# Moving the transposes of W2 from TensorE to the DMA engines, beside a stream of loads

## The chip, the cores and the metric

The kernel runs on one core of a Trainium2 chip. The metric is the device time of one execution, in microseconds (us); smaller is better. The profile's span is a little shorter than this time: 172.3 us of span go with about 174 us. A run is called slow when it lies over 1.5% above the fastest of the same kernel, and ratios use fast runs alone.

## The reference, cut to what matters

Sinkhorn-normalised block attention for four items of 8 heads and 768 tokens, followed by a maxout layer:

```python
x = attention(q, k, v, sort_net)      # (3072 tokens, 512)
h1 = x @ w1                           # w1, w2: (512, 1024)
h2 = x @ w2
g = np.maximum(h1, h2)
out = g @ w_out                       # w_out: (1024, 512)
```

The kernel uses max(h1, h2) = h2 + relu(h1 - h2). So it needs only relu(x (W1 - W2)) for every token, and x (W2 Wout) for the rest. W2 Wout is a 512x512 product that is made once; its left operand must stand in memory as W2 transposed.

## The kernel before

These are the parts that the change and the argument touch. An engine that waits holds up what stands behind it in its own program, as VectorE's first g shows in the result below (45.72 us, behind the turns of v at 43.44). All loads are issued by GpSimd, in one queue; they cast float32 to bf16 on the way.

```python
load_v(0, 0, 3)
...
load_k(0); load_q(0)
load_w_columns(w2_sb, moe_w2, 0, 2)        # W2, first half of the columns
load_w_columns(w1_sb, moe_w1, 0, 1)
load_w_columns(w1_sb, moe_w1, 1, 2)
load_w_columns(w2_sb, moe_w2, 2, 4)        # W2, second half
load_w_columns(w1_sb, moe_w1, 2, 4)        # the last columns of W1
load_w(wo_sb, moe_w_out)
load_v(1)                                  # item 1
w_difference(0, nc.gpsimd)                 # W1 - W2, first quarter
load_k(1)
```

The transposes of W2 are 32 TensorE instructions in two groups, each with one eviction from PSUM, and the product reads the result:

```python
def w2_transposes(t, eng):
    ps = ps_bf16("tw_ps")
    for n in range(16):
        fb, dmt = t * 4 + n // 4, n % 4
        nc.tensor.matmul(ps[:, n * 128 : (n + 1) * 128],
            w2_sb[:, dmt, fb * 128 : (fb + 1) * 128], ident, is_transpose=True, ...)
    return lambda: evac(w2T[:, t * 4 : t * 4 + 4, :]..., ps, 2048, two_x=True, eng=eng)

def w_product(dmt, eng=None):              # one of four "W products"
    for fb in range(NFB):                  # NFB = 8
        nc.tensor.matmul(wc_ps[0][...], w2T[:, fb, dmt * 128 : (dmt + 1) * 128],
                         wo_sb[:, fb, :], ...)
```

For item 0 the order of units is: h of the first half of the tokens, two W products, h of the second half (four products, `moe_h(0, 1, 0..3)`), the other two W products, then the output products. `turn` brings item 1's v into another layout on VectorE in eight pieces; each waits for the load of v.

The softmax here doesn't subtract the row's maximum and nothing guards it: scores larger than these inputs give would overflow.

## Time and profile before

| | before |
|---|---|
| time, median (lowest to highest) | 173.39 us (172.95 to 173.56, 3 runs) |
| TensorE busy | 161.7 us, 94% of the span |
| loads | 12.58 MB written, stream full from 3 to 57 us |
| TensorE transposes of W2 | 32, in two groups of about 1 us |
| DMA transposes (x and q of items 1 to 3) | 16, all after 59 us |

The chain of waits says which engine the end was waiting for, step by step, as shares of the span:

```profile
PE 79%; DMA 7%; ACT 6%; POOL 2%; DVE 2%; issue 2%; ACTq 0%; POOLq 0%
```

PE is TensorE. It is the bound, and DMA stands only for the first load of q.

### The profile page before, as it was taken

The page shows a single profiled execution, that of the slowest core. Times are in us where ns is not written, and L with a number is a line of the kernel's source. Part 1 is how long each engine was busy: PE and PEld are TensorE (multiplying, and loading weights), DVE is VectorE, ACT ScalarE, POOL GpSimd, SP SyncE. Part 2 cuts the span into 40 slices and gives each one's busy share as a digit, 9 for nine tenths or more (in the row PEclk, how much of TensorE's full clock was granted, in tenths as well). Part 3 has the DMA queues.
Part 4 walks back from the last instruction along what each step waited for, and adds up shares of the span by engine and source line. Part 5 has one row for each costly group of instructions (what it writes and reads, how often), then busy time and mean ns, then how long its engine had stood idle before and what let it go on. Part 6 is the DMA issues. An engine that isn't in the chain of part 4 may idle for free.

```text
span 172.3 us, 4531 instructions
## 1 busy us (share of the span) xinstructions
PE 161.7 (94%) x1997; PEld 98.1 (57%) x2015; DVE 88.4 (51%) x194; ACT 83.8 (49%) x101; POOL 24.5 (14%) x40
## 2 busy tenths in 40 slices
PE   7899999989999999998989899999999999999990
PEld 7847766735666555456655445575554546654470
DVE  5879677679656399810685255044452422320130
ACT  4599875864745554069971532465605404312000
POOL 7953362251300000000600000000000000000000
PEclk9999999999999999999999999999999999999998
DMA  3999999999999352993497549920035173000342
GB/s 49 201 206 207 199 207 210 207 205 207 220 212 199 60 167 51 166 233 122 58 203 117 101 135 203 182 109 4 0 51 147 37 198 125 0 0 0 122 183 65
DMA packets 29811, 23.11 MB, mean 134 GB/s; under 512 B 16672, under 2 KB 24736, under 8 KB 29792
## 3 DMA queue, kind: packets, MB, share of 16 engines
q0 software_dynamic: 10304, 12.58, 42.9%
q1 hardware_dynamic: 19200, 10.04, 23.2%
q8 instruction: 16, 0.26, 0.6%
q10 hardware_dynamic: 288, 0.20, 0.4%
q14 instruction: 3, 0.02, 0.0%
HBM read 25.17 MB, written 6.29 MB: 183 GB/s over the span
## 4 chain that ended last, share of the span: by engine, by line
PE 79%; DMA 7%; ACT 6%; POOL 2%; DVE 2%; issue 2%; ACTq 0%; POOLq 0%
PE out_ps L603 36%; PE h_ps L576 24%; DMA q_raw<-in_q_dram 7%; PE o_ps L473 5%; PE wc_ps L554 4%; PE s_ps L446 3%; PE k_ps L379 2%; ACT kT L104 2%; ACT g L590 1%; DVE g L592 1%; ACT w2T L104 1%; PE tw_ps L531 1%; PE tq_ps L349 1%; PE tq_ps L354 1%; POOL k_raw L145 1%
## 5 line engine op out<-in xcount | busy, mean ns | idle before, releaser
L603 PE MATMUL out_ps<-wo_sb,g 128*128 128x512 bf16 (+2 forms) x197 | 47.0, 362 | 1.1 <-ACT o L104 0.5
L576 PE MATMUL h_ps<-xT,w_sb 128*128 128x384 bf16 x256 | 44.8, 326 | 0.8 <-DVE g L592 0.6
L576 PEld LDWEIGHTS <-w_sb 128*128 128x128 bf16 x256 | 24.2, 97 | 16.3 <-issue 0.6
L454 ACT ACTIVATE e<-s_ps 96x768 bf16<-96x768 f32 x32 | 24.2, 807 | 15.8 <-PE s_ps L446 15.7
L603 PEld LDWEIGHTS <-g 128*128 128x128 bf16 x208 | 17.7, 97 | 15.9 <-issue 0.5
L590 ACT ACTIVATE g<-h_ps 128x768 bf16<-128x768 f32 x22 | 17.8, 813 | 16.4 <-PE h_ps L576 16.4
L104 ACT COPY o<-out_ps 128x1024 f32<-128x1024 f32 x10 | 10.1, 1012 | 31.4 <-PE out_ps L603 31.4
L603 PE MATMUL out_ps<-wc,xT 128*128 128x512 bf16 (+2 forms) x103 | 24.9, 362 | 0.1
L490 DVE TENSOR_TENSOR x<-o_ps,rs 96x512 bf16<-96x512 f32 x32 | 22.0, 687 | 1.1
L592 DVE TENSOR_SCALAR g<-h_ps 128x768 bf16<-128x768 f32 x10 | 9.6, 958 | 15.9 <-PE h_ps L576 15.6
L484 DVE RECIPROCAL rs<-o_ps 96x8 f32<-96x8 f32 x32 | 6.4, 201 | 21.7 <-PE o_ps L473 21.5
L603 PEld LDWEIGHTS <-xT 128*128 128x128 bf16 x104 | 9.9, 97 | 11.0
L211 DVE COPY v_dc<-v_raw 64x768 bf16<-64x768 bf16 (+2 forms) x18 | 15.5, 902 | 0.4 <-DMA v_raw<-in_v_dram 0.3
L473 PEld LDWEIGHTS <-e 96*128 96x128 bf16 x256 | 11.6, 97 | 6.6 <-DVE x L490 0.5
L106 DVE CAST v_sb<-v_ps 96x1024 bf16<-96x1024 f32 x7 | 8.5, 1215 | 11.8 <-PE v_ps L421 8.4
L473 PE MATMUL o_ps<-v_sb,e 96*128 96x65 bf16 x256 | 13.1, 193 | 0.1
L104 ACT CAST v_sb<-v_ps 96x1024 bf16<-96x1024 f32 x9 | 8.7, 1014 | 2.0 <-PE v_ps L400 1.9
L446 PEld LDWEIGHTS <-kT 64*128 64x128 bf16 x256 | 6.0, 94 | 6.2 <-issue 4.2
L446 PE MATMUL s_ps<-qT,kT 64*128 64x96 bf16 x256 | 8.7, 204 | 0.7 <-ACT kT L104 0.6
L104 ACT CAST kT<-k_ps 128x1024 bf16<-128x1024 f32 x9 | 8.6, 1021 | 0.7 <-PE k_ps L379 0.7
L82 PEld LDWEIGHTS <-fill 128*128 128x128 bf16 x109 | 7.6, 128 | 2.2 <-DVE fill L73 1.2
L554 PE MATMUL wc_ps<-wo_sb,w2T 128*128 128x512 bf16 x29 | 7.4, 380 | 0.7 <-ACT w2T L104 0.5
(76 smaller groups left out, 130.0 us busy)
## 6 DMA issues: line engine op xcount, KB each, us to landing
out_dram<-o SPq DMA_DIRECT2D x11, 512.0 KB, 3.0
k_raw<-in_k_dram POOLq DMA_DIRECT2D x12, 256.0 KB, 10.4
q_raw<-in_q_dram POOLq DMA_DIRECT2D x4, 768.0 KB, 12.6
v_raw<-in_v_dram POOLq DMA_DIRECT2D x6, 384.0 KB, 13.6
w_sb<-in_moe_w_dram POOLq DMA_DIRECT2D x3, 512.0 KB, 15.9
wo_sb<-in_moe_w_out_dram POOLq DMA_DIRECT2D x2, 512.0 KB, 19.4
v_raw<-in_v_dram POOLq DMA_DIRECT2D x3, 256.0 KB, 4.9
w_sb<-in_moe_w_dram POOLq DMA_DIRECT2D x2, 256.0 KB, 14.3
```

What stands on the lines that cost most here:

```text
L104: nc.scalar.copy(out=out_ap, in_=in_ap)
L106: nc.vector.tensor_copy(out=out_ap, in_=in_ap)
L211: nc.vector.tensor_copy(out=dst, in_=src)
L446: nc.tensor.matmul(ps[:, h2 * 512 + ii * 128 : h2 * 512 + ii * 128 + BLK], kT[b][rows, (hp * 8 + i) * BLK : (hp * 8 + i) * BLK + 128], rhs ...
L454: nc.scalar.activation(out=e[:, 0 : 8 * BLK].rearrange("p (t c r) -> p t c r", t=8, r=R), in_=ps[0:BLK].rearrange("p (t f) -> p t f", t=8) ...
L473: nc.tensor.matmul(ps[:, h2 * 512 + ii * 65 : h2 * 512 + (ii + 1) * 65], e[:, (h2 * 4 + ii) * BLK : (h2 * 4 + ii) * BLK + 128], v_sb[:, m0 ...
L490: nc.vector.tensor_tensor(out=x, in0=ov[:, :, :, 0:D], in1=rs.to_broadcast([BLK, 2, 4, D]), op=ALU.mult,)
L554: nc.tensor.matmul(wc_ps[0][:, m * 512 : (m + 1) * 512], w2T[:, fb, dmt * 128 : (dmt + 1) * 128], wo_sb[:, fb, :], start=(fb == 0), stop=( ...
L576: nc.tensor.matmul(h_ps[t][:, m * 512 : m * 512 + TCH], w1_sb[:, hp, fb * 128 : (fb + 1) * 128], xT[:, b % 2, ch, hp % 2, hp // 2, :], sta ...
L590: nc.scalar.activation(out=g, in_=src, func=AF.Relu)
L592: nc.vector.tensor_scalar(out=g, in0=src, scalar1=0.0, scalar2=None, op0=ALU.max)
L603: nc.tensor.matmul(dst, g_tiles[b, ch, m // 2][:, m % 2, off : off + 128] if m < NFB else xT[:, b % 2, ch, hp % 2, hp // 2, off : off + 12 ...
```

## The change

Its intent is to take 32 transposes off the bounding engine, and two evictions off VectorE and ScalarE. W2 is transposed by eight DMA transposes on the SP queue, which has nothing else to do then. Since they land later, all four W products move behind item 0's h products. The rest spreads the turns of v over the new units and drops a loop that ran once.

```diff
-    w2T = big.tile([128, NFB, DMODEL], BF16, tag="w2T", name="w2T")
+    w2T = big.tile([128, HP, NFB, 128], BF16, tag="w2T", name="w2T")
-    def w2_transposes(t, eng):
-        ... (16 TensorE transposes into PSUM, one eviction)
+    def w2_transposes(t):
+        for dmt in range(HP):
+            nc.sync.dma_start_transpose(
+                out=w2T[:, dmt, t * 4 : t * 4 + 4, :],
+                in_=w2_sb[:, dmt, t * 512 : (t + 1) * 512],
+            )
...
-    w2_out = w2_transposes(0, "D")
-    w2_out()
+    w2_transposes(0)
+    w2_transposes(1)
...
         3: [
             VA[6],
-            lambda: w2_transposes(1, "A")(),
             VA[7],
             lambda: x_transposes(0, 2, "A"),
+            lambda: x_transposes(0, 3, "A"),
             lambda: [turn(second, c) for c in (0, 12, 24)],
         ],
-        4: [lambda: x_transposes(0, 3, "A"), load_rest, lambda: turn(second, 36)],
+        4: [load_rest, lambda: turn(second, 36), lambda: turn(second, 48)],
... (the other turns one unit earlier)
-        if b == 0:
-            units += wps[:2]
         units += [lambda t=t: moe_h(b, 1, t) for t in range(4)]
         if b == 0:
-            units += wps[2:]
+            units += wps
```

More of the change, by code (lines that the diff above doesn't have):

```diff
@@ L12 @@
 BF16 = mybir.dt.bfloat16
-TWICE = 1
 @with_exitstack
@@ L206, in turn_v @@
         src = v_raw[rows].rearrange("p (c d) -> p d c", d=D)[:, d0:d1, c0:c1]
-        for _ in range(TWICE):
-            if eng == "A":
-                nc.scalar.copy(out=dst, in_=src)
-            else:
-                nc.vector.tensor_copy(out=dst, in_=src)
+        if eng == "A":
+            nc.scalar.copy(out=dst, in_=src)
+        else:
+            nc.vector.tensor_copy(out=dst, in_=src)
     rowsum = const.tile([G, NB], FP32, tag="rowsum", name="rowsum")
@@ L521, in x_transposes @@
         evac(xT[:, b % 2, ih, hh], src, 2 * TCH, eng=eng)
-    w2T = big.tile([128, NFB, DMODEL], BF16, tag="w2T", name="w2T")
+    w2T = big.tile([128, HP, NFB, 128], BF16, tag="w2T", name="w2T")
     wc = big.tile([128, HP, DMODEL], BF16, tag="wc", name="wc")
-    def w2_transposes(t, eng):
-        ps = ps_bf16("tw_ps")
-        for n in range(16):
-            fb, dmt = t * 4 + n // 4, n % 4
-            nc.tensor.matmul(
-                ps[:, n * 128 : (n + 1) * 128],
-                w2_sb[:, dmt, fb * 128 : (fb + 1) * 128],
-                ident,
-                is_transpose=True,
-                start=True,
-                stop=True,
-            )
-        return lambda: evac(
-            w2T[:, t * 4 : t * 4 + 4, :].rearrange("p f d -> p (f d)"),
-            ps,
-            2048,
-            two_x=True,
-            eng=eng,
-        )
+    def w2_transposes(t):
[3 more added lines that the diff above has]
+                in_=w2_sb[:, dmt, t * 512 : (t + 1) * 512],
+            )
     wc_ps = {}
@@ L555, in w_product @@
                 wc_ps[0][:, m * 512 : (m + 1) * 512],
-                w2T[:, fb, dmt * 128 : (dmt + 1) * 128],
+                w2T[:, dmt, fb, :],
                 wo_sb[:, fb, :],
@@ L716 @@
             VA[6],
-            lambda: w2_transposes(1, "A")(),
             VA[7],
             lambda: x_transposes(0, 2, "A"),
+            lambda: x_transposes(0, 3, "A"),
             lambda: [turn(second, c) for c in (0, 12, 24)],
         ],
-        4: [lambda: x_transposes(0, 3, "A"), load_rest, lambda: turn(second, 36)],
-        5: [lambda: block_diagonals(1), lambda: turn(second, 48)],
-        6: [lambda: turn(second, 60)],
-        7: [lambda: turn(second, 72)],
-        8: [lambda: turn(second, 84)],
+        4: [load_rest, lambda: turn(second, 36), lambda: turn(second, 48)],
+        5: [lambda: block_diagonals(1), lambda: turn(second, 60)],
+        6: [lambda: turn(second, 72)],
+        7: [lambda: turn(second, 84)],
         9: [
@@ L754 @@
         if b == 0:
-            units += wps[2:]
-            cost[4:4] = [1.7] * 2
-            cost += [1.7] * 2
+            units += wps
+            cost += [1.7] * 4
         units += [
```

## The prediction

> **What bounds the kernel now.** I first read the page's busy shares and slices, to see which engine is full and until when memory is.
>
> ```profile
> PE 161.7 (94%) x1997; PEld 98.1 (57%) x2015; DVE 88.4 (51%) x194; ACT 83.8 (49%) x101; POOL 24.5 (14%) x40
> ...
> PE   7899999989999999998989899999999999999990
> ...
> DMA  3999999999999352993497549920035173000342
> GB/s 49 201 206 207 199 207 210 207 205 207 220 212 199 60 167 51 166 233 122 58 203 117 101 135 203 182 109 4 0 51 147 37 198 125 0 0 0 122 183 65
> ```
>
> TensorE is busy 94% of 172.3 us, so the end moves by TensorE work removed minus TensorE idle added. One slice is 4.3 us: the DMA engines are full up to about 56 us. So loads are the second bound there. The 200 to 220 GB/s are bytes as written in bf16; the loads cast from float32, so twice that is read (the page: 25.17 MB read, 12.58 MB moved by the load queue).
>
> Then I read the timeline of 16 to 44 us, where the changed work sits.
>
> ```profile
> 25.10 0.80 ACT L104 COPY xT<-tx_ps 128x768 bf16<-128x768 bf16 x1 [0.54 <-PE tx_ps L511]
> 25.42 1.04 PEld L531 LDWEIGHTS <-w_sb 128*128 128x128 bf16 x16
> ...
> 26.68 1.23 DVE L106 COPY w2T<-tw_ps 128x2048 bf16<-128x2048 bf16 x1 [1.81 <-PE tw_ps L531]
> ...
> 27.82 0.68 DVE L191 TENSOR_TENSOR w_sb<-w_sb 128x1024 bf16<-128x1024 bf16 x1
> ...
> 28.56 1.48 PE L576 MATMUL h_ps<-xT,w_sb 128*128 128x384 bf16 x8
> ...
> 32.47 1.06 PE L531 MATMUL tw_ps<-ident,w_sb 128*128 128x128 bf16 x16
> ...
> 33.56 1.87 ACT L104 COPY w2T<-tw_ps 128x2048 bf16<-128x2048 bf16 x1 [0.33 <-PE tw_ps L531]
> ...
> 35.07 3.04 DVE L211 COPY v_dc<-v_raw 64x768 bf16<-64x768 bf16 x4 [0.34 <-DMA v_raw<-in_v_dram]
> ...
> 35.48 1.04 PE L554 MATMUL wc_ps<-wo_sb,w2T 128*128 128x512 bf16 x4 [0.51 <-ACT w2T L104]
> ...
> 38.66 5.37 PE L576 MATMUL h_ps<-xT,w_sb 128*128 128x384 bf16 x32
> ...
> 40.38 0.96 DVE L592 TENSOR_SCALAR g<-h_ps 128x768 bf16<-128x768 f32 x1
> ```
>
> The reader is to see three things. Both W2 transposes cost TensorE about 1 us each, and their evictions 1.23 us of VectorE and 1.87 us of ScalarE. The third h product starts at 28.56, just after the W1 - W2 difference that it reads ended at 27.82 + 0.68 = 28.50. And VectorE's turning of item 1's v starts at 35.07 because v has only just landed. In the trace's landing records the last W1 columns land at 27.13 and v's first half at 35.05, so two consumers have almost no slack.
>
> The third view was the DMA issues, for what a transpose by DMA costs here.
>
> ```profile
> xT<-x SPq DMA_TRANSPOSE x12, 2.9
> ...
> qT<-q_pair SPq DMA_TRANSPOSE x4, 4.0
> ```
>
> **What the Trainium skill says.** "DMA: Bandwidth & Descriptors", section "Issuing engines are not separate DMA queues": transfers issued from SP and from GpSimd run on the same 16 engines and interleave. Its section "Queues, rings and completion order" has each engine go round its queues packet by packet. Before's trace has no moment with transposes beside a full load queue, so it can't confirm either. "Advanced Engine Details and Errata", section "X-Bar Transpose (TRN2)", says such transposes are as fast as regular DMAs, 350 to 400 GB/s. This trace disagrees: an x transpose of 768 packets of 256 B (197 KB) takes 1.15 us from first to last packet, 171 GB/s, and a packet 18 ns (median). "TensorE: Matmul & The Clock Gate", section "Part 4: PE-mode transpose", gives about 275 ns in a kernel for 128x128; here each lasts 217 ns, but 16 take only 1.06 us because they overlap. So what is removed is small.
>
> **The change, part by part.**
>
> *Removed.* 32 TensorE transposes: 0.89 and 0.91 us on the chain, 1.8 us. The stall of 0.51 us before the second four W products. 3.1 us of evictions, which no longer stand before the W1 - W2 difference and the xT eviction.
>
> *The first saving does not reach h.* Without the first 16 transposes, TensorE goes on after the xT eviction ends (25.10 + 0.80 = 25.90) instead of at 26.48: 0.55 us early, so it would reach the third h product at 28.0. But W1's last columns land at 27.13, the difference takes 0.7, so the product is allowed at about 27.95. There is no room for a later landing.
>
> *The second saving is lost in the new order.* Values 6 and 7 now follow each other, then both x transposes, then h at once. VectorE needs 0.9 us (0.2 reciprocal, 0.69 product) for each of the two x. Call T the start of the third h product. From the rows before, TensorE ends values 6 at T + 4.05, values 7 at T + 4.4, the first x transposes at T + 4.9; VectorE ends the second x at T + 5.95, so TensorE idles 1.1 us; the transposes end at T + 6.5, their eviction on ScalarE at T + 7.35, and the third matmul of h waits 0.55 us for it. The W products, which covered this eviction, are gone from here. h of the second half (four of 1.33 us) ends at T + 12.4, two W products (16 x 0.217 = 3.5) at T + 15.9, sorting k at T + 17.6, the third W product at T + 19.3. With T = 28.0 that is 47.3; before, TensorE stood at the same point at 47.42. So if the transposes cost the loads nothing, the change is worth about 0.1 us here. I worked out the choice of engine by the kernel's own load counter; it shifts a few evictions (all three kT of item 1 to ScalarE), worth some tenths either way.
>
> *Added: 1 MB by DMA amid the loads.* Eight transposes of 128x512: 512 packets each, 4096 in all, 256 per engine. At 18 to 25 ns a packet (25 is the pace of the two q transposes back to back, 3072 packets in 4.8 us) this is 4.6 to 6.4 us of every engine. If only the read side is short, 1 MB at the loads' read rate of 410 GB/s is 2.4 us. I choose 3 to 4. The first four can go when W2's first half has landed (19.38), the others when the second half has (24.55, later itself): all compete before v's first half lands.
>
> *On the path.* Half the delay, d1 = 1.5 to 2, shifts the last W1 columns, so T becomes 29.5 to 30. All of it, dv = 3 to 4, shifts v: the turning starts at 38 to 39. Three turns (2.35 us) now stand before the first g of the second half on VectorE, so this g ends at 38.5 + dv. The fourth h product needs its PSUM buffer (four in the ring) and gets there at T + 11.1 = 39.0 + d1. Further stall: dv - d1 - 0.5. Sum: the loss is the larger of d1 - 0.1 and dv - 0.6, which for dv = 3 is 2.4 us, for 4 is 3.4. Later everything is TensorE-bound and shifts along. The later loads' consumers (q of item 1 lands at 43.97, k at 40.02) come after the shifted W products and don't add.
>
> **Rivals.**
>
> (a) *The transposes slip between the loads.* If engines mostly wait for HBM, the loads lose under 1 us and the time is 173 to 174. For: packets of loads overlap in one engine (their durations sum to 1.2 times the slices). Against: the GB/s row is flat near 205 for packets from 512 to 4096 B, a rate that looks like a ceiling.
>
> (b) *The transposes starve.* If an engine alternates one small packet with one load packet (6144 B for v), the loads lose less early, but the last transposes land after 50 us and the last W products (50.05 before, some 52 then) wait: 177 to 179. For: the load queue is never empty up to 56 us. Against: the loads of W and q have short packets, so most transposes would pass with them.
>
> (c) *A gain.* The 1.8 us of TensorE work comes off in full and the x chain is hidden: 171.5. For: TensorE is the bound. Against: both savings end in front of a landing and a VectorE chain just computed. Over 2% (3.5 us) is more than all that is removed (1.8 + 0.5).
>
> **Range and chances.** The main line gives 173.4 + 2.4 to 3.4, about 176. Rival (a) and partial overlap pull it down; since the author re-spread the turns to suit, I lean that way and say 175.3. The range goes from (a)'s good end to (b)'s middle, 172.9 to 178.2. Slower by over 2% needs above 176.9, that is dv above 4 or (b): 0.28. Faster by over 2%: 0.02. The rest: 0.70.
>
> **What would show it.** Right: the transposes' landing times spread over 22 to 35 us; the last W1 columns land at 28.5 or later and the third h product starts behind them; VectorE's first turn waits for v until 37 to 39; a TensorE gap before the x transposes and before the fourth h product. Wrong: v landing within 1 us of 35.05, or W products waiting for w2T, or TensorE idle falling in 25 to 45 us.

## More of the kernel before

The next view gives, for stretches of the kernel, each engine's busy time in us and the number of its instructions, the granted clock of TensorE (1.00 is full), the busy share of the DMA engines (over 1 where packets overlap) and the GB/s that they moved:

```profile
core 0: us, PE busy (x) PEld busy (x) DVE busy (x) ACT busy (x) POOL busy (x), PEclk, DMA share, GB/s
...
44.00:56.00 12.00, 11.49 (x233) 8.09 (x236) 7.21 (x9) 6.99 (x8) 1.58 (x2) 1.00 1.11 210
56.00:68.00 12.00, 11.89 (x129) 6.18 (x130) 9.23 (x18) 6.40 (x8) 0.00 (x0) 1.00 0.43 99
68.00:76.00 8.00, 7.94 (x56) 4.08 (x56) 5.47 (x17) 1.97 (x3) 0.00 (x0) 1.00 0.96 190
```

TensorE is all but full in each stretch, at the full clock; in the first stretch the loads move at 210 GB/s. One row of the same timeline, the sorting of item 1's v (start and duration in us), serves as a mark for the comparison below:

```profile
47.43 1.57 PE L400 MATMUL v_ps<-bd,v_dc 64*128 64x64 bf16 x48
```

## The result

| | before | after |
|---|---|---|
| time, median | 173.47 us (172.95 to 173.8) | 198.8 us (197.99 to 199.17) |
| ratio | 1 | 1.1457 (95%: 1.1409 to 1.1504) |
| mean granted clock | 0.996 | 0.947 |

A ratio is the mean time of one kernel's fast runs over that of the other's of the same rounds, so not quite the ratio of the two medians. The change costs 25 us, and the predicted range ended at 178.2.

The page of the changed kernel: busy shares, then the slices of the span (each 4.9 us here; PEclk is TensorE's granted clock in tenths).

```profile
PE 167.1 (85%) x1983; PEld 98.1 (50%) x1983; DVE 87.1 (44%) x193; ACT 82.1 (42%) x100; POOL 23.2 (12%) x40
...
PE   7799969635670199999998899899999999999993
...
PEclk9999999985999556999999999999999999999999
DMA  4999999999999991033992792497202227200223
GB/s 71 206 200 202 206 170 198 142 130 133 198 190 188 99 110 25 0 91 100 174 196 88 112 202 51 146 177 183 95 3 41 44 106 186 106 3 0 106 87 125
...
PE 57%; DMA 19%; SPq 12%; ACT 5%; POOL 2%; issue 1%; DVE 1%; ACTq 0%; POOLq 0%
PE out_ps L589 32%; PE h_ps L562 14%; SPq L528 12%; DMA w2T<-w_sb 12%; DMA w_sb<-in_moe_w_dram 7%; PE o_ps L471 3%; PE wc_ps L540 3%; ACT kT L103 2%; PE s_ps L444 2%; PE v_ps L398 1%; ACT g L576 1%; PE tq_ps L347 1%; DVE g L578 1%; POOL k_raw L144 1%; POOL v_raw L153 1%
```

The damage lies between 25 and 75 us. The DMA row is full (9) to the fifteenth slice, as if much were moved, yet GB/s falls from 200 to 142, 130 and 133: the DMA engines had packets under way all the time and moved less. The last two lines are the chain of waits: the issue of the transposes on SP and their transfer, 12% each, have come into it, 24% of 197 us. Stretch by stretch, against the same stretches of before:

```profile
44.00:56.00 12.00, 6.59 (x24) 2.58 (x23) 7.72 (x14) 0.81 (x1) 2.44 (x5) 0.75 1.31 170
56.00:68.00 12.00, 2.88 (x102) 1.90 (x100) 0.44 (x1) 3.76 (x4) 0.93 (x1) 0.82 1.22 161
68.00:76.00 8.00, 7.67 (x69) 5.03 (x70) 3.40 (x3) 1.01 (x1) 0.00 (x0) 0.50 1.19 90
```

From 56 to 68 us TensorE works 2.9 us of 12. From 68 to 76 it looks busy again (7.67 of 8), but at a clock of 0.50: its matmuls take twice as long. The timeline names what it waited for (start, duration, engine, line, operation, output and inputs; in brackets the idle time before and what ended it):

```profile
19.74 32.33 SPq L528 DMA_TRANSPOSE w2T<-w_sb  x8
...
29.61 1.47 PE L562 MATMUL h_ps<-xT,w_sb 128*128 128x384 bf16 x8 [1.75 <-DVE w_sb L190]
...
35.74 0.51 PE L509 MATMUL tx_ps<-ident,x 96*128 96x96 bf16 x8 [1.27 <-DVE x L488]
...
43.44 2.25 DVE L209 COPY v_dc<-v_raw 64x768 bf16<-64x768 bf16 x3 [7.75 <-DMA v_raw<-in_v_dram]
...
45.72 0.96 DVE L578 TENSOR_SCALAR g<-h_ps 128x768 bf16<-128x768 f32 x1
...
46.73 2.72 PE L562 MATMUL h_ps<-xT,w_sb 128*128 128x384 bf16 x8 [5.61 <-DVE g L578]
...
55.24 1.04 PE L540 MATMUL wc_ps<-wo_sb,w2T 128*128 128x512 bf16 x4 [1.86 <-DMA w2T<-w_sb]
...
68.33 1.89 PE L540 MATMUL wc_ps<-wo_sb,w2T 128*128 128x512 bf16 x4 [9.44 <-DMA w2T<-w_sb]
...
70.15 2.74 PE L398 MATMUL v_ps<-bd,v_dc 64*128 64x64 bf16 x48
```

Two waits stand out. First, v of item 1 lands at 43.4 us instead of 35.05, VectorE turns it late, the first g of the second half stands behind these turns, and TensorE waits 5.61 us for that g's PSUM buffer. Second, the third W product waits 9.44 us for its transposed W2. The sorting of v, which began at 47.43 before, begins at 70.15 and takes 2.74 us instead of 1.57. From there on the two kernels do the same work.

The trace also holds every packet of the DMA engines and every landing. The following is worked out from these records (the packets of the load queue and of the transposes that start in each stretch of 4 us; 4-byte packets left out):

```
us            before: loads            after: loads             after: transposed
              packets  GB/s            packets  GB/s            packets (256 B each)
26 to 30      806      208             594      152             579
34 to 38      397      204             131      136             150
50 to 54      312      200             545      163             536
58 to 62       20        4             120      171             147
66 to 70        0        0             194       56             198

landing, us              before   after
last columns of W1        27.13    28.77
v of item 1, first half   35.05    43.41
q of item 1               43.97    55.39
v of item 3, last         55.02    72.33
the eight transposes         -    28.65 32.08 41.88 48.19 51.43 55.20 68.28 73.85
```

In every stretch the transposes get about as many packets as the loads, whether a load packet is 1024 B (26 to 30) or mostly 6144 B (34 to 38, 58 to 62). Their share of the bytes falls with this from 20% to 7% (579 packets of 256 B beside 152 GB/s, 150 beside 136 GB/s). There are 4096 transposed packets. The 4096th load packet after the first of them starts at 72.7 us, and the last transpose has landed at 73.85. So the transposes advance one packet for each load packet, and a stretch of long load packets starves them.

A second thing shows in the landings. Each of the 16 engines reports its own share. For the second half of Wout the first engine was done at 33.04 and the last at 41.48, 8.4 us apart (before: 30.30 and 33.52). The third transpose, in the same period, landed on all 16 between 40.39 and 41.88; of the other seven, four landed within 0.3 us and none was spread over more than 1.9. This suggested the first theory below: the transposes go in step over all engines, at the pace of the one that is furthest behind in its loads.

### The profile page after: what moved, and what is told of

It is laid out like the page before. It is cut to its first block, busy times and chain, and to the rows that moved or that the text cites. A ratio compares the mean times of both kernels' runs of the same rounds, so it can differ in the third digit from the quotient of the medians.

```text
span 197.3 us, 4495 instructions
## 1 busy us (share of the span) xinstructions
PE 167.1 (85%) x1983; PEld 98.1 (50%) x1983; DVE 87.1 (44%) x193; ACT 82.1 (42%) x100; POOL 23.2 (12%) x40
## 4 chain that ended last, share of the span: by engine, by line
PE 57%; DMA 19%; SPq 12%; ACT 5%; POOL 2%; issue 1%; DVE 1%; ACTq 0%; POOLq 0%
PE out_ps L589 32%; PE h_ps L562 14%; SPq L528 12%; DMA w2T<-w_sb 12%; DMA w_sb<-in_moe_w_dram 7%; PE o_ps L471 3%; PE wc_ps L540 3%; ACT kT L103 2%; PE s_ps L444 2%; PE v_ps L398 1%; ACT g L576 1%; PE tq_ps L347 1%; DVE g L578 1%; POOL k_raw L144 1%; POOL v_raw L153 1%
## 5 line engine op out<-in xcount | busy, mean ns | idle before, releaser
L562 PE MATMUL h_ps<-xT,w_sb 128*128 128x384 bf16 x256 | 46.5, 332 | 9.0 <-DVE g L578 6.2
L589 PE MATMUL out_ps<-wo_sb,g 128*128 128x512 bf16 (+2 forms) x208 | 48.3, 363 | 0.5 <-ACT o L103 0.5
L452 ACT ACTIVATE e<-s_ps 96x768 bf16<-96x768 f32 x32 | 24.2, 807 | 17.3 <-PE s_ps L444 17.2
L576 ACT ACTIVATE g<-h_ps 128x768 bf16<-128x768 f32 x21 | 17.0, 812 | 24.1 <-PE h_ps L562 24.1
L103 ACT COPY o<-out_ps 128x1024 f32<-128x1024 f32 x9 | 9.1, 1012 | 31.3 <-PE out_ps L589 31.3
L578 DVE TENSOR_SCALAR g<-h_ps 128x768 bf16<-128x768 f32 x11 | 10.5, 956 | 25.9 <-PE h_ps L562 24.6
L540 PE MATMUL wc_ps<-wo_sb,w2T 128*128 128x512 bf16 x32 | 10.8, 485 | 12.1 <-DMA w2T<-w_sb 12.1
L103 ACT CAST v_sb<-v_ps 96x1024 bf16<-96x1024 f32 x9 | 8.8, 1037 | 12.5 <-PE v_ps L398 12.0
L540 PEld LDWEIGHTS <-w2T 128*128 128x128 bf16 x32 | 3.5, 120 | 17.9 <-DMA w2T<-w_sb 13.6
L103 ACT CAST kT<-k_ps 128x1024 bf16<-128x1024 f32 x11 | 10.5, 1025 | 0.7 <-PE k_ps L377 0.7
```

Source lines behind the costliest of these rows:

```text
L103: nc.scalar.copy(out=out_ap, in_=in_ap)
L452: nc.scalar.activation(out=e[:, 0 : 8 * BLK].rearrange("p (t c r) -> p t c r", t=8, r=R), in_=ps[0:BLK].rearrange("p (t f) -> p t f", t=8) ...
L540: nc.tensor.matmul(wc_ps[0][:, m * 512 : (m + 1) * 512], w2T[:, dmt, fb, :], wo_sb[:, fb, :], start=(fb == 0), stop=(fb == NFB - 1),)
L562: nc.tensor.matmul(h_ps[t][:, m * 512 : m * 512 + TCH], w1_sb[:, hp, fb * 128 : (fb + 1) * 128], xT[:, b % 2, ch, hp % 2, hp // 2, :], sta ...
L576: nc.scalar.activation(out=g, in_=src, func=AF.Relu)
L578: nc.vector.tensor_scalar(out=g, in0=src, scalar1=0.0, scalar2=None, op0=ALU.max)
```

## The experiments

Theory 1: transposed packets and load packets take turns one by one, the transposes go in step over the 16 engines, and so both streams suffer. Its rivals: the new order itself costs (2); only the wait for the late transposes costs (3); the transposes are slow by themselves (4); the transposes get a fixed share of bytes or time (5). All runs gave correct results. Fifteen kernels were run.

### The order alone: order_pe

```diff
 # the changed kernel with the TensorE transposes of before
+    w2_out = w2_transposes(0, "D"); w2_out()          # where before had it
+        3: [VA[6], lambda: w2_transposes(1, "A")(), VA[7], ...]
```

> The changed order, but W2 transposed on TensorE as before. Theory 1 (the transposes share the DMA engines with the loads, one 256 B packet against one load packet, all 16 engines in step, and both streams suffer): no DMA transposes of W2, so the order alone costs little: 173 to 174.5 us, v of item 1 lands near 35 us. Theory 2 (the new order, with the x transposes and h products no longer covered by W products, is what costs): over 180 us.

Measured: 176.02 us (175.24 to 176.79), ratio 1.0144 (1.0097 to 1.0192). Theory 2 is out as the main cause, but 2.5 us is more than I expected. The timeline of the profiled run (176.79 us) shows a part of them:

```profile
36.26 0.48 PE L574 MATMUL h_ps<-xT,w_sb 128*128 128x384 bf16 x2 [0.88 <-ACT xT L103]
36.96 4.11 PE L574 MATMUL h_ps<-xT,w_sb 128*128 128x384 bf16 x14 [0.22 <-ACT xT L103]
```

The 14 matmuls took 4.11 us, where the changed kernel's own took 2.44. The granted clock was 0.57 from 37 to 41 us (in the trace's clock records, 0.5 for 3.41 us from 37.30). It fell after three short waits (0.68, 0.88 and 0.22 us). It did not fall in every run: 176.79 and 176.65 us go with mean clocks of 0.987 and 0.985, 175.40 and 175.24 us with 1.000 and 0.998 (3.41 us at 0.5 take 0.010 from the mean). So the fall costs about 1.4 us where it happens, and without it the order is still 1.8 us slower than before.

### The order, with the waits filled: order_pe_fill

```diff
 # order_pe with matmuls on zeros in the waits
             lambda: x_transposes(0, 2, "A"),
+            lambda: keep_streaming(ps_f32("fill_ps"), 1536),
             lambda: x_transposes(0, 3, "A"),
...
+    moe_h(b, 1, t, n=2048 if b == 0 and t == 0 else 0)   # 2048 columns of zeros first
```

> The changed order with TensorE transposes (176.0 us) plus matmuls on zeros in the short waits before the last x transposes (1536 columns) and before the first h product of the second half (2048 columns). If the order lost its 2.5 us mostly to the granted clock, which fell to half for some 4 us after these waits: 173.3 to 174.5 us. If to the waits themselves: unchanged, 175.5 to 176.5.

Measured: 174.34 us (174.25 to 174.35 in the three fast runs; a fourth took 574.29 us, which the profile doesn't explain, and is left out as slow), ratio 1.0046.

```profile
33.75 0.81 PE L81 MATMUL fill_ps<-fill 128*128 128x512 bf16 x3
34.59 0.51 PE L509 MATMUL tx_ps<-ident,x 96*128 96x96 bf16 x8
34.94 1.03 PE L81 MATMUL h_ps<-fill 128*128 128x512 bf16 x4
...
36.69 2.44 PE L574 MATMUL h_ps<-xT,w_sb 128*128 128x384 bf16 x14 [0.22 <-ACT xT L103]
```

The matmuls on zeros (line 81) do nothing but keep TensorE busy, and the 14 matmuls are back at 2.44 us. Of the 2.5 us that the order costs, the filling wins 1.7 back, and 0.8 stay. Not all of the 1.7 is the clock: the two runs of order_pe whose clock did not fall are still 1.0 us slower than the filled ones, which the record doesn't explain.

### The slowed loads alone: before_plus_dma

```diff
 # the kernel before, plus
+    w2X = big.tile([128, HP, NFB, 128], BF16, tag="w2X", name="w2X")
     w2_out()
+    w2_dma(0); w2_dma(1)      # the eight DMA transposes of the change, into w2X, which nobody reads
```

> The kernel before, whole, plus the eight DMA transposes into a tile that nobody reads. Theory 1: nobody waits for the transposes, but the loads still lose; v of item 1 lands after 42 us instead of 35, and the time is 183 to 190 us, most but not all of the 25 us. Theory 2 (the order): 173 to 174 us. Theory 3 (only the late landing of the transposes costs, through the W products that wait for them; the loads' delay hides): 173 to 175 us.

Measured: 181.8 us in the one fast run, which has the profile; 186.71, 187.26 and 187.29 in three that count as slow beside it (clocks 0.976, 0.972, 0.972 and 0.959). There is no ratio for this reason. In the fast run alone the loss is 8 us, a little under the range expected, in the others within it; v of item 1 landed at 40.48 us in the profiled run, earlier than the 42 expected. Every run shows a loss that theories 2 and 3 exclude. What sets the runs apart isn't known: 181.8 and 186.71 us have nearly the same clock. VectorE's first turn of v:

```profile
40.51 3.01 DVE L211 COPY v_dc<-v_raw 64x768 bf16<-64x768 bf16 x4 [4.92 <-DMA v_raw<-in_v_dram]
```

Before, this row started at 35.07.

### Plain copies instead of transposes: before_plus_copy

```diff
 # before_plus_dma, but
-            nc.sync.dma_start_transpose(out=w2X[:, dmt, t * 4 : t * 4 + 4, :], ...)
+            nc.sync.dma_start(
+                out=w2X[:, dmt, t * 4 : t * 4 + 4, 0:128],      # rows of 144, so 256 B pieces
+                in_=w2_sb[:, dmt, t * 512 : (t + 1) * 512].rearrange("p (f d) -> p f d", d=128),
+            )
```

> before_plus_dma with plain copies on the same queue in place of the transposes: the same bytes, cut into the same 4096 packets of 256 B. If what hurts the loads is sharing the engines packet by packet: as before_plus_dma, 181 to 187 us, v of item 1 after 40 us. If it is the transposes' going in step over all 16 engines: the loads lose only the copies' own time, about 26 ns per packet and engine, v of item 1 lands at 37 to 39, and 174.5 to 179 us.

Measured: 176.14 us (175.87 to 178.26), ratio 1.0185 (1.0112 to 1.0258), so slower, but by 2% or not is unclear.

```profile
37.56 3.04 DVE L211 COPY v_dc<-v_raw 64x768 bf16<-64x768 bf16 x4 [2.52 <-DMA v_raw<-in_v_dram]
```

The copies also go one packet for one: 615 to the loads' 611 in 26 to 30 us, 204 to 179 in 34 to 38. They too are starved: the last lands at 62.88. But the loads lose far less. v of item 1 lands at 37.54 instead of 40.48 with transposes (35.05 without either), and the last v of item 3 at 61.01 instead of 67.71. v's first half landed within 2.5 us over the 16 engines (35.08 to 37.54) with copies, within 5.0 us (35.50 to 40.48) with transposes. So taking turns costs the loads 2.5 us by then, and it is a property of transposes, beyond sharing, that doubles the delay and pulls the engines apart. It isn't that their packets take longer: from 26 to 34 us a packet of either took 31 ns (median). But from 38 to 42 us a 2048 B load packet took 221 ns in the mean beside transposes, and 172 ns beside copies, as without either. And the copies' own landings follow each engine: the seventh was spread over 6.4 us (52.65 to 59.07), the seventh transpose in before_plus_dma over 1.6 (58.69 to 60.25). Going in step explains all this; the records don't name the engine of a packet, so no run shows it directly.

### The waits of the change, one taken away: after_g_act

```diff
 # the changed kernel, but
-        units += [lambda t=t: moe_h(b, 1, t) for t in range(4)]
+        units += [lambda t=t: moe_h(b, 1, t, "A" if b == 0 and t == 0 else None) for t in range(4)]
```

> The changed kernel with the first g of item 0's second half evicted by ScalarE instead of VectorE, so that it does not stand behind the turning of the late v. Theory 1: the idle of 5.6 us before the fourth h product goes, but the third W product still waits for its transpose, which lands near 68 us, so the time stays within 1.5 us of the changed kernel (197 to 199.5). If the waits add up instead: about 193 us.

Measured: 198.24 us (197.9 and 198.58), ratio 1.1425. The wait of 5.61 us before the fourth h product is gone (h ends at 42.4 instead of 49.4), and nothing is won:

```profile
46.96 1.87 PE L540 MATMUL wc_ps<-wo_sb,w2T 128*128 128x512 bf16 x4 [4.56 <-DVE pm L295]
...
67.31 1.89 PE L540 MATMUL wc_ps<-wo_sb,w2T 128*128 128x512 bf16 x4 [8.46 <-DMA w2T<-w_sb]
```

The third W product (second row) waits for its transposed W2 as before. The waits don't add up; the one that ends last sets the time.

### The slowed loads and the order, without the wait for W2: order_pe_plus_dma

```diff
 # order_pe, plus the eight idle DMA transposes into w2X of before_plus_dma
```

> The changed order with TensorE transposes (176.0 us), plus the eight DMA transposes into a tile nobody reads. If most of the 25 us is the W products' wait for the transposes: 182 to 188 us, the 8 to 14 us that the slowed loads cost in the order of before, on top of 176. If the slowed loads alone do it in this order: 193 to 199 us.

Measured: 182.52 and 183.99 us in the fast runs, 185.62 and 188.42 in two slow ones; median 184.8, ratio of the fast ones 1.057 (1.05 to 1.0641). v of item 1 lands at 41.21, the last transpose at 71.79, much as in the changed kernel, but nobody waits for it. The ratios give the sum of the whole loss: the order 1.4%, the slowed loads 5.7 - 1.4 = 4.3%, and the W products' wait for the transposes, with the fallen clock behind it, 14.6 - 5.7 = 8.9%. More than half of the loss is the wait for the transposes. The sizes are rough: with the two slow runs counted in, the slowed loads come to about 5.3% and the wait to 7.8%.

### No loads beside the transposes: after_paused

```diff
 # the changed kernel; the transposes are issued as each half of W2 lands; behind W2's second half
+    pause = const.tile([1, HP], BF16, tag="pause", name="pause")
+    for dmt in range(HP):
+        nc.gpsimd.tensor_copy(out=pause[:, dmt : dmt + 1], in_=w2T[0:1, dmt, 4, 0:1])
     load_w_columns(w1_sb, moe_w1, 2, 4)      # this and all later loads come after
```

> The changed kernel with no loads beside most of the transposes: the second half of W2 is loaded, then GpSimd holds back all further loads until the eight transposes have landed. Theory 1: once the loads ahead of them have drained, a transpose takes 2 to 3 us from issue to landing and the eight are done by about 34 us; no W product waits for them; the loads behind start some 6 to 9 us late; 179 to 185 us. Theory 4 (these transposes are slow by themselves, whatever else the DMA engines do): each still takes over 5 us, the eight over 35 us, and with the loads behind them the time is over 200 us.

Measured: 186.34 us (185.8 to 187.8, five fast runs), ratio 1.0744. The tile's view of w2T gives the time from issue to landing:

```profile
DMA to landing us min/median/max: 2.4/3.6/7.3
```

The same line of the changed kernel reads 8.9, 21.1 and 26.3 us. Once the loads had landed (24.6 us), the transposes landed at 26.75 to 32.84, and no W product waited for them: the first four, which were queued by then, 0.5 us apart (26.75, 27.23, 27.71, 28.22), the rest one every 1.3 us, the pace at which SP issued them (an issue took 1.27 us, median). Theory 4 is out. The time is just above the range expected, and this is my doing: holding back the last columns of W1 as well made TensorE wait 11.7 us for them.

```profile
PE h_ps L563 <- DVE w_sb L187: 11.7, 1, 11.7
```

### Half of the transposes: after_half

```diff
 # the changed kernel, but t = 1 on TensorE (16 transposes and one eviction on ScalarE, before VA[7])
-    w2_transposes(1)
+            lambda: w2_transposes_pe(1, "A"),
```

> The changed kernel with only the first four transposes by DMA (2048 packets); the other half of W2 is transposed on TensorE, as before. Theory 1: the four are through when about 2048 load packets have passed since 23 us, that is in the load of item 1's k, near 42 to 46 us, so no W product waits long; v of item 1 still lands near 43 us, as the loads up to there are accompanied all the same, so the wait before the fourth h product stays (4 to 6 us); 181 to 185 us. If the loss were in proportion to the bytes transposed: about 186 us, with v of item 1 landing near 39.

Measured: 181.04 and 181.31 us (fast) and 185.12 (slow), ratio 1.0442 (1.0407 to 1.0477). The profiled run is the slow one; its landings are given for what they show of the order of events. The four transposes landed at 28.54, 31.97, 40.88 and 48.02 (the last was expected near 42 to 46), v of item 1 at 43.2, as late as with all eight, and once the transposes were through, the loads went back to 183 to 218 GB/s. The turns by count hold.

### Smaller load packets: after_v_small and before_v_small, and mended ones

```diff
 # both kernels: v of items 1 to 3 in eight pieces of 1536 B per row instead of two of 6144 B
-    load_v(1)
+    load_v(1, 0, 8)           # likewise load_v(2, 0, 8) and load_v(3, 0, 8)
```

> The changed kernel with v of items 1 to 3 loaded in eight pieces instead of two: packets of 1536 B instead of 6144 B, four times as many, the same bytes. Theory 1 (one transposed packet goes per load packet, all engines in step): the same 4096 transposed packets now find their partners earlier, and no engine holds the others up with a 6144 B packet, so the last transposes land near 52 to 60 us instead of 68 and 74, and the time falls to 182 to 189 us. Theory 5 (the transposes get a fixed share of the bytes or of the time, whatever the loads' packets): within 2 us of the changed kernel, 197 to 201.

> The control for after_v_small: the kernel before with the same smaller packets of v. All theories: 172.5 to 175 us, within 1% of before.

Measured: 190.31 us (189.68 to 190.61) and, for the control, 187.55 us (186.94 to 188.59). The control failed: with more loads to issue, GpSimd came to its W1 - W2 difference only after 33 us, and TensorE waited 12.5 us for it. The pair says nothing in us. The edit was mended by moving that difference ahead:

```diff
     load_w(wo_sb, moe_w_out)
-    load_v(1, 0, 8)
     w_difference(0, nc.gpsimd)
+    load_v(1, 0, 8)
     load_k(1)
```

> As after_v_small, mended: GpSimd now does its W1 - W2 difference before it issues item 1's v, so that the many small loads don't hold it back. Theory 1 (one transposed packet per load packet, engines in step): the last transposes land near 52 to 60 us instead of 68 and 74, no W product waits over 3 us, 180 to 188 us. Theory 5 (a fixed share of bytes or time, whatever the packets): 197 to 201.

> The control for after_v_small2, mended in the same way: 172.5 to 175.5 us by all theories. If it is far off again, the pair says nothing in us, only in landing times.

Measured: 178.85 and 180.41 us (fast) and 184.07 (slow), ratio 1.0353 (1.0291 to 1.0415); the control 173.64 us, ratio 1.0007. Four times as many packets for the same bytes take back three quarters of the loss, without touching a transpose. But the records show a second reason: from 38 to 42 us only 92 load packets started, as GpSimd issued the next loads late (it waited for the load of Wout until 37.47), and 2085 transposed packets went through in this gap. The last transpose landed at 45.57. Where both queues were full they went one for one again (572 and 575 in 30 to 34 us).

### Packets of 3072 B: after_v_4 and before_v_4

The same edit with four pieces, so that GpSimd has fewer loads to issue.

> The changed kernel with v of items 1 to 3 in packets of 3072 B instead of 6144 B, twice as many, GpSimd's difference ahead of them. Theory 1 (one transposed packet per load packet, engines in step): with 128 more partners per item and shorter ones, the seventh transpose lands some 3 to 8 us before 68 us, the third W product starts as much earlier, 190 to 196 us. If only a gap in the load queue helped before: 197.5 to 200 us.

> The control for after_v_4, with the same smaller packets in the kernel before: 173 to 174.5 us by all theories.

Measured: 186.61 and 189.25 us (fast), 189.43 and 190.68 (slow), ratio 1.084; the control 174.2 and 175.01 us. This is faster than expected (190 to 196). In the profiled run, a slow one, the seventh transpose landed at 55.66 instead of 68.28. However, the load queue thinned out here too (149 load packets against 720 transposed ones in 42 to 46 us). So the same bytes in other packets change the time by 5 to 10%, but these runs don't separate how much came from smaller packets and how much from the gaps, and the times alone don't decide on theory 5. The counts do: a fixed share of the bytes doesn't fit 20% and 7%, nor a fixed share of the time packets that took 1.1 us of each engine's 4 us from 26 to 30 us, and 0.7 from 34 to 38.

### The clock in the changed kernel: after_fill

```diff
 # the changed kernel
+            if dmt == 2: keep_streaming(wc_ps[0], 18432)     # before the third W product
+    moe_h(b, 1, t, n=10240 if b == 0 and t == 2 else 0)
```

> The changed kernel with matmuls on zeros in TensorE's two long waits (20 of 512 columns before the third h product of the second half, 36 before the third W product), shorter than the waits, so that nothing is held up. If the granted clock falls because TensorE idles, and matmuls then take twice as long: the clock stays up after the waits and the time falls by 2 to 4 us, to 195 to 197. If the clock doesn't matter: unchanged, 198 to 199.

Measured: 191.21 us (fast), 195.5, 196.18 and 199.62 (slow beside it, clocks 0.99, 0.99 and 0.974), median 195.84. The times fall with the mean clock, but with one fast run the size can't be given. In the profiled run, the slowest, the sorting of v behind the filled wait was back at its full pace, 1.57 us instead of 2.74:

```profile
69.41 1.57 PE L398 MATMUL v_ps<-bd,v_dc 64*128 64x64 bf16 x48
```

There the fourth W product then waited for the eighth transpose (75.73 us) instead.

No version beats the kernel before. The nearest, order_pe_fill, is 0.5% slower; the transposes have no place where the loads leave the DMA engines free before W2 Wout is needed (the loads end at 59 us, the first product that reads W2 Wout starts at 55.5).

## Why the prediction was wrong

**The bound and what is removed** held. TensorE's 32 transposes and the two evictions went, worth about 2 us.

**The timeline of the new order** held almost row by row. It said that the third h product would be started by W1's last columns at T = 29.5 to 30 (measured 29.61), that TensorE would idle 1.1 us before the second x transposes (1.27) and 0.55 us before the third matmul of h (0.56). The sum that the order alone is worth about nothing was 2.5 us too hopeful (order_pe), 1.8 in the runs whose clock did not fall. That the clock would fall after these short waits was not in the sum.

**The added DMA work is the step that failed.** "I choose 3 to 4" us of delay, from bytes and from packet durations. Two terms of this were wrong.

The first is how much the loads lose. By W1's last columns they had lost 1.6 us, as predicted (1.5 to 2), but by v's first half 8.4 us, not 3 to 4. The sum charged v for all 4096 packets; only 1736 had started when v landed, and they cost more than it gave them. With plain copies, 1589 had started and the loads had lost 2.5 us, so that this is near 3 to 4 is chance; all the copies together cost the last v of item 3 6.0 us (61.01 against 55.02), within the sum's 4.6 to 6.4. The eight transposes cost it 12.7 us in the order of before and 17.3 in the changed kernel. What transposes do beyond sharing was not in the sum. The mechanism behind it held, with the larger number in it: the sum "dv - d1 - 0.5" gives 8.4 - 1.6 - 0.5 = 6.3 us of stall for the fourth h product, and 5.61 were measured. Its loss, dv - 0.6, becomes 7.8 us; the rest of the 25 is not in the main line.

The second, and the larger, is how long the transposes take to land: the W products waited for them, 9.44 us before the third, which the main line did not foresee. Rival (b), that they alternate with load packets and starve, was the right one. It was set aside with "most transposes would pass with" the short packets of W and q. This could have been counted: in the trace of before, counted from 23.65 us (the first transposed packet of the changed kernel), the 2048th load packet starts at 38.7 us and the 4096th at 55.4, even with the loads at full speed. Rival (b) named landings after 50 us and 177 to 179 us for this; the true landings, 68.28 and 73.85, come from both terms together, since the slowed loads bring their packets, the transposes' partners, later too.

**"Later everything is TensorE-bound and shifts along"** held in kind, but at half clock for some us after each wait. The sorting of v was 22.7 us late and the end 25 us.

What stays open: how much of the 25 us is the clock (after_fill points to a few us and is not clean), and what in the transposes makes the loads lose more than with copies of the same packets. Going in step fits the landings and the copies; it was argued from them, not seen. Nor is it known why before_plus_dma and order_pe_plus_dma scatter by 5 to 6 us from run to run.

## What to carry to other kernels

When two DMA streams share the engines, count packets, not bytes: a stream of small packets beside a full load queue lands when as many load packets have passed. Move work to an idle-looking queue only where its engines are idle. Where a transpose runs beside loads that are on the path, don't take its cost from a copy of the same packets: here the loads lost 5.4 us by item 1's v with transposes, 2.5 with copies. Before a wait is accepted on TensorE, look at what it does to the granted clock after it: several short waits close together were enough in order_pe.

## What the Trainium skill lacked or had wrong

- "DMA: Bandwidth & Descriptors", section "Queues, rings and completion order", has an engine drain a whole packet, typically about 9 to 17 descriptors, before it goes to the next queue. The traces agree that the queues take turns, and add that the turns are equal in what the profile counts as packets, whatever their size: 579 transposed to 594 loaded (1024 B), 150 to 131 (mostly 6144 B). How many of them pass in one turn the counts don't show. The section lacks what follows for a queue of small packets: its share of the bytes fell from 20% to 7%.
- The same page, section "Rules for kernel authors", says that a transpose next to ordinary DMAs needs nothing. For the results this holds in all runs. It lacks the cost: with plain copies of the same packets the kernel took 176.14 us, with transposes 181.8 to 187.29 us, and v of item 1 landed over 5.0 us on the 16 engines instead of 2.5.
- "Advanced Engine Details and Errata", section "X-Bar Transpose (TRN2)", expects 350 to 400 GB/s. With no loads beside them (after_paused), queued transposes of 128x512 (131 KB) landed 0.48 to 0.51 us apart, about 265 GB/s.
- "TensorE: Matmul & The Clock Gate", section "What's actually happening", has the clock fall after an idle window of about 3.4 us. In these traces the window need not be idle. The clock records start and end on a grid of 3.41 us. In the 17 traces, cut on this grid, the clock fell from 1.0 to 0.5 in 23 places, each time right after a stretch of 3.41 us in which TensorE's matmuls were busy for 48% or less (in order_pe 48%, with waits of 0.68, 0.88 and 0.22 us). Where it stayed at 1.0, the stretch before was busy for 50% or more, but for five of 45 to 49%.
